# A fused recurrence and soft mixture of experts: the epsilon and the maximum's spread by reduces, slot factors on ScalarE, and identity transposes from less idle time on

## The chip, the cores and the metric

The kernel runs on one core of a Trainium2 chip. The metric is the device time of one execution in microseconds. Engines are called as in the profile: PE (TensorE; PEld its weight loads), DVE (VectorE), ACT (ScalarE), POOL (GpSimd), SP (SyncE, which issues the transfers). L1703 is line 1703 of the kernel before.

## The reference

Two layers, one behind the other. Cut to what matters:

```python
# 1. gated linear recurrence, x, r_gate, i_gate: 4 x 5056 x 256
a_t = np.exp(8.0 * sigmoid(r_gate) * np.log(clip(sigmoid(a_param))))
x_g = np.sqrt(np.maximum(1.0 - a_t * a_t, 1e-06)) * sigmoid(i_gate) * x
h = a_t[:, t] * h + x_g[:, t]          # over the 5056 steps of each batch; y[:, t] = h
# 2. soft mixture of experts over the 20224 tokens y, 8 experts x 4 slots = 32 slots
logits = y @ phi
d = np.exp(logits - logits.max(0)); d /= d.sum(0) + 1e-09      # over tokens
slot_input = d.T @ y
slot_out[e] = np.maximum(slot_input[e] @ w1[e], 0.0) @ w2[e]   # hidden width 1024
c = np.exp(logits - logits.max(1)); c /= c.sum(1) + 1e-09      # over slots: the combine
out = c @ slot_out
```

## The kernel before, in words

The 20224 tokens are cut into 40 pieces q of 512 (the last has 256), and the pieces into units p of one or two; channels lie on partitions in two halves h. For each piece, SP loads the tiles of r, i and x (Dr, Di, Dx); TensorE transposes r (TR, L879); ScalarE takes its tanh (SR, L887); an exponential makes the decay (EX, L994); GpSimd squares it (SQ, L976); ScalarE takes the root (RT, L1016) and the tanh of i (SI, L928); GpSimd multiplies gate and x (U, L956); TensorE transposes the products (TU, L1061); VectorE combines them (ST, L1077) and runs the scan (SC, L1094). TensorE then transposes the result back (TY, L1126), VectorE or ScalarE copies it out of PSUM (YC, L1141 or L1139; the last pieces in halves, L1167), and for groups g of up to four pieces TensorE computes the logits (LG), which are kept, and accumulates the slot inputs (AC, L1304) under a running maximum per group position (LE; AE adds into accS; DM is the factor for an older maximum).

When the last group is in, a thread of small steps joins the four rows of partial maxima and sums: MT transposes the maxima, MX (L1512) takes the maximum over the four, MR (L1514) spreads it over four places, MC (L1516) brings it back to the partitions by a product, WJ (L1518) subtracts, WE (L1521) takes the exponential, W (L1522) multiplies a constant 0/1 matrix R by it, SP0 and SP1 (L1528) join the sums with W, DN (L1542) the denominator, SL (L1539) copies the slots out. RD (L1546 to L1548) takes the reciprocal of the denominator and multiplies R by it to R2, which is used after the second expert layer (RS). L1.0 to L1.7 (L1583) and L2.0 to L2.7 (L1631) are the expert layers; HS and HR stand between them; HZ (L1559) and SZ (L1497) are memsets of their padded operands on GpSimd.

The combine weights are made for each group g: CT (L1681) transposes the logits to tokens on partitions, CM and CS (L1692, L1695) take off the maximum, CE (L1698) is the exponential, RR sums the slots (L1702), adds 1e-9 (L1703) and takes the reciprocal (L1704), CN (L1709) multiplies on GpSimd. Then HP (L1747) transposes, HE copies, OT (L1775) multiplies by the experts' outputs, OE (L1789 on ScalarE, L1791 on VectorE) copies the result out, and OD (L1806) stores it.

The order of the tasks on each engine is written out by hand (ORDER). A planner walks through these lists with a duration for each task, gives out the buffers at its planned times, and puts in identity transposes (two of a constant matrix, L1455; "fillers") where TensorE has nothing to do: up to the planned time 200 and again from 250 to 275, if a PSUM buffer is to spare. Up to 250 it also takes the last free buffer once a count of idle time is over the first number of DEBT; the count is capped by the second number, and TensorE's work pays it off at the rate of the third:

```python
self.debt = min(DEBT[1], self.debt + max(0.0, now - free_at[e]))
self.debt = max(0.0, self.debt - DEBT[2] * (extra + dur))
...
t = self.filler(now, now < self.warm_again and self.debt + now - free_at[e] > DEBT[0])
```

SHARED names the tasks on VectorE that the planner holds until GpSimd is free, and during which it holds GpSimd. SPX adds to the planned duration of single transfers on SP. Neither is an instruction. On VectorE the list around the thread is "LE11 LD11 AE9 MX MR RR2 WJ YC39.1 W AE11a AE11b CM4 SL CS4 RD RR4 RR1", on TensorE "TE10 TY39.1 MC AC10.0 AC10.1 AC11.0 CT4 SP0 SP1 DN L1.0", on ScalarE "ES11 YC39.0 WE DM10 CE4 HS0 HS1".

Of the kernel before, what the change touches and what calls it, by code (L numbers as in the profile page):

```python
# [16 lines left out]
P = 128  # L17
# [105 lines left out]
        EX18.1 DM6 YC28.0 SI37 DM8 RT18.0 YC30.0 YC29.0 RT20.0 YC31.0 YC29.2 RT19.0 YC32.0 ES8 YC34.0 CE1 YC33.0 YC35.0 YC38.0 YC37.0 YC36.0  # L123
        DM9 ES9 YC38.1 YC37.1 ES10 ES11 YC39.0 WE DM10 CE4 HS0 HS1 SO0 SO1 SH0 SH1 HE1.8 HE1.0 OE0.0 OE0.3 OE0.2 OE1.0 OE1.2 CE3 OE1.10
        HE2.0 HE2.8 OE1.11 CE11 OE1.9 OE2.0 OE2.3 CE8 OE2.1 OE2.8 OE2.9 HE4.0 OE2.11 CE5 OE2.10 HE4.8 OE4.0 OE4.1 OE4.2 CE10 OE3.0 OE3.3
# [10 lines left out]
        ST16.0 YC26.0 SC16.0 ST16.1 ST17.0 SC16.1 SC17.0 LE8 ST17.1 AE6 SC17.1 AE7 ST18.0 ST18.1 SC18.0 SC18.1 ST19.0 ST19.1 SC19.0 AE8 LE9  # L136
        SC19.1 ST20.1 ST20.0 SC20.1 SC20.0 LE10 RR0 LE11 LD11 AE9 MX MR RR2 WJ YC39.1 W AE11a AE11b CM4 SL CS4 RD RR4 RR1 HR0 HR1 HE0.0 CM3
        CS3 OE0.1 OE1.1 OE1.3 OE1.8 CM11 CS11 CM8 CM5 CS8 RR3 OE2.2 CS5 CM10 CM7 HE3.0 CS7 RR11 CS10 OE4.3 RR5 OE3.2 RR10 HE5.8 CM9 HE5.0
# [19 lines left out]
COLD = 5.5  # L158
DEBT = (1.2, 1.6, 0.8)

TT = 0.0622
HP = 64
SHARED = ("W", "MR", "RD", "U0", "SQ0.0", "SQ0.1")
RSEED = 523661183.0
# [51 lines left out]
class Planner:  # L216
# [158 lines left out]
    def run_fixed(self, orders):  # L375
# [32 lines left out]
        def begin(t, e):  # L408
            nonlocal n
            for b in t.alloc:  # L410
                self.take(b)
            dur, extra = t.alt.get(e, t.dur), 0.0
            if e == "PE":
                if self.shape is not None and t.shape != self.shape:
                    extra = SWITCH
                self.shape = t.shape
                if now < COLD:
                    dur *= 2
                self.debt = min(DEBT[1], self.debt + max(0.0, now - free_at[e]))
                self.debt = max(0.0, self.debt - DEBT[2] * (extra + dur))  # L420
            if e == "ACT" and t.kind and self.table not in KIND[t.kind]:
                extra = LOAD
                self.table = KIND[t.kind][0]
            if t.name == "LN":
                self.table = "exp"
            t.start, t.eng_used = now, e
            free_at[e] = now + extra + dur
            t.end = free_at[e] + t.lat
            order.append(t)
            n += 1  # L430
            heapq.heappush(finish, (t.end, n, t))

        while n_done < len(self.tasks):
# [17 lines left out]
            while again:  # L451
                again = False
                for e in engines:
# [12 lines left out]
                    if e == "PE" and (self.warm_from <= now < self.warm_to or self.warm_again <= now < self.warm_end):  # L466
                        t = self.filler(now, now < self.warm_again and self.debt + now - free_at[e] > DEBT[0])
                        if t is not None:
                            begin(t, e)
# [127 lines left out]
def kernel(  # L597
# [126 lines left out]
    def e_const():  # L724
# [777 lines left out]
    def merge_tasks():  # L1502
        small = {}
        if tc is not None:
            for nm, sh in (("mmax", [1, 1, NS]), ("mrep", [1, J, NS]), ("wj", [P, 1]), ("W", [P, J, NS]),
# [7 lines left out]
            out=small["mmax"][:, 0, :], in_=t(mp)[:1, :P].rearrange("o (j s) -> o s j", s=NS), axis=AX.X, op=ALU.max))  # L1513
        a = add("DVE", "MR", 0.21, deps=[a], prio=-60, emit=lambda: nc.vector.tensor_copy(  # L1514
            out=small["mrep"], in_=small["mmax"].broadcast_to([1, J, NS])))
        a = add("PE", "MC", 0.3, deps=[a], prio=-60, uses=[mp], shape="R", emit=lambda: nc.tensor.matmul(  # L1516
            t(mp)[:, P : P + 1], small["mrep"].rearrange("o j s -> o (j s)"), ones, start=True, stop=True))
        a = add("DVE", "WJ", 0.15, deps=[a], prio=-60, uses=[mp], emit=lambda: nc.vector.tensor_tensor(  # L1518
            out=small["wj"], in0=mm, in1=t(mp)[:, P : P + 1], op=ALU.subtract))
        a = add("ACT", "WE", 0.1, deps=[a], prio=-60, kind="exp",  # L1520
                emit=lambda: nc.scalar.activation(small["wj"], small["wj"], AF.Exp))  # L1521
        w = add("DVE", "W", 0.3, deps=[a, t_const2], prio=-60, emit=lambda: nc.vector.tensor_scalar(  # L1522
            small["W"], R, small["wj"], None, op0=ALU.mult))
        sp = Buf("one", "sp")
# [142 lines left out]
    def mk_c(g, first):  # L1667
# [177 lines left out]
```

## Time and profile before

| | us |
|---|---|
| median of 3 runs | 290.21 (290.15 to 290.63) |
| the profiled execution | 289.1 |
| its span, first to last instruction | 287.2 |
| busy PE / DVE / ACT / POOL | 247.3 / 233.1 / 236.1 / 189.7 |
| mean granted clock of TensorE | 0.988 of full |

The span is what the trace shows; the 1.9 us around it are launch and end. A busy share is a mean over stages with different limits, so the stages have to be read one by one. TensorE's busy time holds the fillers (L1455, 310 instructions).

### The profile page before, as it was taken

To read this page: it belongs to the slowest core of one execution; us is meant where nothing else is said; L and a number is where in the kernel's file an instruction comes from. 1 tells how busy PE (TensorE), PEld (TensorE's weight loads), DVE (VectorE), ACT (ScalarE), POOL (GpSimd) and SP (SyncE) were. 2 spreads that over 40 slices of the span, in tenths; PEclk is the share of its full clock that TensorE was granted. 3 is DMA by queue.
4 is the path that set the end of the run, shared out by engine and by line. 5 is a ranking of instruction groups with operands and counts; after the bars stand their busy time and mean duration, and the time that the engine had idled before them with its cause. 6 is when DMAs were issued, how large, how long until landed. Compare 5 with 4: busy or idle time off the path is not lost. (4 is left out here: it accounts for less than half of the span.)

```text
span 287.2 us, 9134 instructions
## 1 busy us (share of the span) xinstructions
PE 247.3 (86%) x3915; PEld 182.0 (63%) x3915; DVE 233.1 (81%) x275; ACT 236.1 (82%) x258; POOL 189.7 (66%) x144
## 2 busy tenths in 40 slices
PE   8978978998879879777987978989989999889980
PEld 7767665865645856656656746456545687667880
DVE  0896499999999999999999999999982189974600
ACT  7879999999999999999999999997511199868600
POOL 1458969999999999979999999991514002420000
PEclk9979999999999999999999999999999999999997
DMA  6999999999997799999899997999992069998995
GB/s 198 403 410 401 408 376 411 407 404 407 407 408 283 226 389 388 346 321 406 288 338 369 379 390 232 400 400 402 394 386 85 2 256 413 415 415 333 412 418 234
DMA packets 27421, 100.25 MB, mean 349 GB/s; under 512 B 3058, under 2 KB 3060, under 8 KB 24948
## 3 DMA queue, kind: packets, MB, share of 16 engines
q1 hardware_dynamic: 27376, 99.66, 89.8%
q8 instruction: 31, 0.51, 0.7%
q14 instruction: 10, 0.08, 0.1%
q10 hardware_dynamic: 4, 0.00, 0.0%
HBM read 78.94 MB, written 20.71 MB: 347 GB/s over the span
## 5 line engine op out<-in xcount | busy, mean ns | idle before, releaser
L956 POOL TENSOR_TENSOR b<-b 128x1024 f32<-128x1024 f32 x38 | 89.5, 2381 | 4.7 <-ACT b L928 4.2
L1094 DVE TENSOR_TENSOR_SCAN b<-b,pair 128x1024 f32<-128x1024 f32 (+8 forms) x48 | 92.3, 1948 | 0.2
L976 POOL TENSOR_TENSOR b<-b 128x1024 f32<-128x1024 f32 (+2 forms) x41 | 73.5, 1814 | 15.3 <-ACT b L994 14.6
L1077 DVE SCALAR_TENSOR_TENSOR pair<-b,pair 128x1024 f32<-128x1024 f32 (+2 forms) x42 | 48.1, 1156 | 5.6 <-ACT b L1016 3.8
L1061 PE MATMUL pair<-ident,b 64*128 64x64 f32 x1112 | 43.5, 226 | 5.9 <-ACT b L887 2.0
L1061 PEld LDWEIGHTS pair<-ident,b 64*128 64x128 f32 x1112 | 38.3, 139 | 13.9 <-issue 4.1
L994 ACT ACTIVATE b<-b,ca 128x2048 f32<-128x2048 f32 (+3 forms) x26 | 42.9, 1683 | 0.1
L887 ACT ACTIVATE b<-pair 128x1024 f32<-128x1024 f32 (+1 forms) x39 | 38.8, 1010 | 2.7 <-PE pair L879 2.7
L879 PE MATMUL pair<-ident,st 64*128 64x64 f32 x616 | 27.4, 230 | 11.3 <-DMA st<-in_r_gate_dram 4.4
L879 PEld LDWEIGHTS pair<-ident,st 64*128 64x128 f32 x616 | 22.5, 140 | 21.3 <-ACT b L887 5.0
L1016 ACT ACTIVATE b<-b 128x2048 f32<-128x2048 f32 (+1 forms) x20 | 35.9, 1842 | 0.1
L1709 POOL TENSOR_TENSOR b<-b,rs_all 128x512 f32<-128x512 f32 (+3 forms) x12 | 10.5, 895 | 37.4 <-DVE rs_all L1704 32.0
L928 ACT ACTIVATE b<-b 128x2048 f32<-128x2048 f32 x17 | 32.5, 1915 | 0.1
L1126 PE MATMUL pair<-ident,b 64*128 64x64 f32 x576 | 25.4, 227 | 7.1 <-DVE b L1094 3.2
L1126 PEld LDWEIGHTS pair<-ident,b 64*128 64x128 f32 x576 | 20.8, 138 | 16.8 <-DVE b L1094 4.6
L1141 DVE COPY yn<-pair 128x1024 f32<-128x1024 f32 x23 | 27.9, 1215 | 2.6 <-PE pair L1126 2.6
L1775 PE MATMUL bank<-eS,yn 32*128 32x256 f32 x238 | 26.4, 403 | 0.8 <-DVE yn L1760 0.4
L1789 ACT COPY b<-bank 128x512 f32<-128x512 f32 x41 | 22.4, 606 | 4.1 <-issue 2.5
L1304 PE MATMUL one<-yn,eS 128*32 128x257 f32 x316 | 24.2, 386 | 0.9 <-DVE yn L1167 0.9
L1455 PE MATMUL one<-ident 128*128 128x128 f32 x144 | 24.2, 284 | 0.3 <-DVE b L1219 0.3
L1206 PE MATMUL one<-b,phi_sb 128*32 128x512 f32 (+1 forms) x164 | 24.3, 581 | 0.0
L1775 PEld LDWEIGHTS bank<-eS,yn 32*128 32x128 f32 x238 | 19.4, 197 | 3.8 <-ACT b L1789 1.5
(156 smaller groups left out, 371.1 us busy)
## 6 DMA issues: line engine op xcount, KB each, us to landing
b<-in_x_dram SPq DMA_DIRECT2D x39, 512.0 KB, 9.0
st<-in_r_gate_dram SPq DMA_DIRECT2D x38, 512.0 KB, 9.1
b<-in_i_gate_dram SPq DMA_DIRECT2D x38, 512.0 KB, 8.5
out_dram<-b SPq DMA_DIRECT2D x19, 1024.0 KB, 6.3
b<-in_moe_w_dram SPq DMA_DIRECT2D x28, 512.0 KB, 8.8
st<-in_moe_w_dram SPq DMA_DIRECT2D x4, 512.0 KB, 7.7
st<-in_r_gate_dram SPq DMA_DIRECT2D x3, 256.0 KB, 2.8
st<-in_i_gate_dram SPq DMA_DIRECT2D x1, 512.0 KB, 5.4
```

Source lines behind the costliest of these rows:

```text
L879: nc.tensor.transpose(out=o[f][:, m, :], in_=v, identity=idn)
L887: nc.scalar.activation(dst, v, AF.Sigmoid if SIGR else AF.Tanh, scale=1.0 if SIGR else 0.5)
L928: nc.scalar.activation(v, v, AF.Tanh, scale=0.5)
L956: eng.tensor_tensor(out=o, in0=a, in1=b, op=ALU.mult)
L976: eng.tensor_tensor(out=o, in0=v, in1=v, op=ALU.mult)
L994: nc.scalar.activation(v, v, AF.Exp, scale=ca[:, h : h + 1], bias=ca[:, h : h + 1])
L1016: nc.scalar.activation(v, v, AF.Sqrt, bias=f, scale=-f)
L1061: nc.tensor.matmul(o[f][:, i * J + m, :], v, idn, is_transpose=True, start=(nm == nms[0] and m == 0 and i == 0), stop=(nm == nms[-1]), ski ...
L1077: nc.vector.scalar_tensor_tensor(v, t(Nb[p])[:, h, :c], 0.5e-3 if gate_of(quads(p)[0]) == "E" else 1e-3, v, op0=ALU.max, op1=ALU.mult)
L1094: nc.vector.tensor_tensor_scan(dst, dst, flat()[:, s0:s1], init, op0=ALU.mult, op1=ALU.add)
L1126: nc.tensor.transpose(out=t(yp)[:, f, (b * H + h) * HP : (b * H + h + 1) * HP], in_=v, identity=idn)
L1775: nc.tensor.matmul(t(ops[x])[:, c * D : (c + 1) * D], t(hT)[r, off : off + (P - 1) * ns + 1 : ns], t(soRb)[r, :D], start=True, stop=True,)
```

## The change

RR's addition of 1e-9 becomes a tensor_reduce: the sum is written beside a constant 1e-9 in a new tile rs_two, and a second reduce adds the pair. MR becomes a tensor_reduce over groups of one element. W leaves VectorE: WE and W become one task on ScalarE, the exponential and a copy of R scaled by it. R2 becomes a task of its own on ScalarE, between HS0 and HS1. In the planner, the count's numbers become 0.3 (limit) and 1.5 (rate) up to the planned time 45, then 1.0 and 1.0, where they were 1.2 and 0.8; W, MR and RD are no longer held for GpSimd; and planned durations of three transfers change.

```diff
-        DM9 ES9 YC38.1 YC37.1 ES10 ES11 YC39.0 WE DM10 CE4 HS0 HS1 SO0 ...
+        DM9 ES9 YC38.1 YC37.1 ES10 ES11 YC39.0 W DM10 CE4 HS0 R2 HS1 SO0 ...
-        SC19.1 ST20.1 ... MX MR RR2 WJ YC39.1 W AE11a AE11b CM4 SL CS4 RD ...
+        SC19.1 ST20.1 ... MX MR RR2 WJ YC39.1 AE11a AE11b CM4 SL CS4 RD ...
-DEBT = (1.2, 1.6, 0.8)
+DEBT = (1.0, 1.6, 1.0)
+DEBT0 = (45.0, 0.3, 1.5)
-SHARED = ("W", "MR", "RD", "U0", "SQ0.0", "SQ0.1")
+SHARED = ("U0", "SQ0.0", "SQ0.1")
-SPX = {("r", 0): 0.21, ("r", "b"): 0.33, ("r", 1): 0.45, ("r", 2): 0.32, ("r", 3): 0.1, ("x", PHI): 1.2}
+SPX = {("r", 0): 0.21, ("r", "b"): 0.33, ("r", 1): 0.45, ("i", 0): 0.55, ("x", PHI): 1.2}
-                self.debt = max(0.0, self.debt - DEBT[2] * (extra + dur))
+                self.debt = max(0.0, self.debt - (DEBT0 if now < DEBT0[0] else DEBT)[2] * (extra + dur))
-                        t = self.filler(now, now < self.warm_again and self.debt + now - free_at[e] > DEBT[0])
+                        t = self.filler(now, now < self.warm_again and self.debt + now - free_at[e] > (DEBT0[1] if now < DEBT0[0] else DEBT[0]))
+        rs_two = sb.tile([P, J * J, 2], F32, name="rs_two")
+        nc.gpsimd.memset(rs_two, 1e-9)
-        a = add("DVE", "MR", ... nc.vector.tensor_copy(
-            out=small["mrep"], in_=small["mmax"].broadcast_to([1, J, NS])))
+        a = add("DVE", "MR", ... nc.vector.tensor_reduce(
+            out=small["mrep"], in_=small["mmax"].rearrange("o j (s k) -> o j s k", k=1).broadcast_to([1, J, NS, 1]), axis=AX.X, op=ALU.max))
-        w = add("DVE", "W", 0.3, ... nc.vector.tensor_scalar(small["W"], R, small["wj"], None, op0=ALU.mult))
+        def e_we():
+            nc.scalar.activation(small["wj"], small["wj"], AF.Exp)
+            nc.scalar.activation(small["W"].rearrange("p j s -> p (j s)"), R.rearrange("p j s -> p (j s)"), AF.Copy, scale=small["wj"])
+        w = add("ACT", "W", 0.42, ... emit=e_we)
-            nc.vector.tensor_scalar(small["R2"], R.rearrange("p j s -> p (j s)"), small["rd"], None, op0=ALU.mult)
+        rd = add("ACT", "R2", 0.25, deps=[rd], ... nc.scalar.activation(
+            small["R2"], R.rearrange("p j s -> p (j s)"), AF.Copy, scale=small["rd"]))
-            nc.vector.tensor_reduce(out=v, in_=cn(), axis=AX.X, op=ALU.add)
-            nc.vector.tensor_scalar(v, v, 1e-9, None, op0=ALU.add)
+            nc.vector.tensor_reduce(out=rs_two[:, :m, 0], in_=cn(), axis=AX.X, op=ALU.add)
+            nc.vector.tensor_reduce(out=v, in_=rs_two[:, :m, :], axis=AX.X, op=ALU.add)
             nc.vector.reciprocal(v, v)
```

## Rows read from the trace of the kernel before

**Rows 1.** Windows of three stages: length, busy time (instructions) by engine, clock, DMA.
```profile
60.00:80.00 20.00, 17.06 (x308) 13.10 (x308) 19.95 (x20) 19.94 (x16) 19.38 (x11) 1.00 1.03 407
...
221.00:229.00 8.00, 8.00 (x131) 4.89 (x124) 0.69 (x3) 0.43 (x2) 0.00 (x0) 1.00 0.01 2
...
259.00:261.00 2.00, 2.00 (x15) 1.52 (x12) 0.59 (x2) 1.56 (x4) 0.00 (x0) 1.00 0.53 221
```

**Rows 2.** Timeline, 204 to 213 us: start, length, engine, line [idle before].
```profile
204.83 0.28 DVE L1702 TENSOR_REDUCE rs_all<-b 128x4 f32<-128x128 f32 x1
...
206.93 0.67 DVE L1702 TENSOR_REDUCE rs_all<-b 128x16 f32<-128x512 f32 x1
...
207.30 1.80 POOL L1559 MEMSET b<- 128x2048 f32 x1
...
207.63 1.97 DVE L1703 TENSOR_SCALAR rs_all<-rs_all 128x16 f32<-128x16 f32 x1
...
208.00 0.38 PE L1516 MATMUL bank<-ones,mrep 1*128 1x1 f32 x2
...
208.32 1.07 PE L1304 MATMUL one<-yn,eS 128*32 128x257 f32 x16
...
209.05 0.52 POOL L1497 MEMSET yn<- 128x512 f32 x1
...
209.63 0.25 DVE L1704 RECIPROCAL rs_all<-rs_all 128x16 f32<-128x16 f32 x1
...
209.80 0.10 DVE L1518 TENSOR_TENSOR wj<-M,bank 128x1 f32<-128x1 f32 x1
...
209.81 0.42 DVE L1167 COPY yn<-bank 128x256 f32<-128x256 f32 x1
...
210.25 0.29 DVE L1522 TENSOR_SCALAR W<-R,wj 128x128 f32<-128x128 f32 x1
...
210.28 0.63 PE L1304 MATMUL one<-yn,eS 128*32 128x257 f32 x4 [0.89 <-DVE yn L1167]
...
210.84 0.75 PE L1681 MATMUL bank<-ident,b 128*128 128x128 f32 x4
...
211.04 0.61 DVE L1338 SCALAR_TENSOR_TENSOR accS<-accS,dm,one 128x128 f32<-128x128 f32 x2 [0.50 <-PE one L1304]
...
211.53 0.60 PE L1528 MATMUL bank<-W,accS 128*64 128x32 f32 x8
```

**Rows 3.** Timeline, 248 to 258 us, the output stage.
```profile
248.49 1.05 POOL L1709 TENSOR_TENSOR b<-b,rs_all 128x512 f32<-128x512 f32 x1 [3.26 <-DVE rs_all L1704]
...
248.92 0.64 DVE L1703 TENSOR_SCALAR rs_all<-rs_all 128x16 f32<-128x16 f32 x1
...
254.73 1.53 PE L1455 MATMUL bank<-ident 128*128 128x128 f32 x12
...
257.40 0.59 ACT L1789 COPY b<-bank 128x512 f32<-128x512 f32 x1 [2.52 <-issue]
```

**Rows 4.** One line, L1141: duration min/median/max in ns, first and last start.
```profile
L1141 DVE COPY yn<-pair x23: 1198/1216/1226, 28.0 to 172.1; 128x1024 f32<-128x1024 f32 x23
```

**Rows 5.** Windows of 1 and 0.5 us at the fall of the clock.
```profile
15.00:16.00 1.00, 0.11 (x4) 0.00 (x0) 0.81 (x2) 1.00 (x2) 1.00 (x1) 1.00 1.00 406
...
18.00:18.50 0.50, 0.50 (x12) 0.50 (x13) 0.47 (x2) 0.40 (x1) 0.10 (x1) 0.50 1.06 426
```

**Rows 6.** Timeline, 17 to 24 us, TensorE and ScalarE.
```profile
16.63 0.71 PE L879 MATMUL pair<-ident,st 64*128 64x64 f32 x16 [1.52 <-DMA st<-in_r_gate_dram]
...
17.90 1.11 PE L879 MATMUL pair<-ident,st 64*128 64x64 f32 x16 [0.56 <-DMA st<-in_r_gate_dram]
...
19.06 1.03 ACT L887 ACTIVATE b<-pair 128x1024 f32<-128x1024 f32 x1 [0.65 <-PE pair L879]
...
19.80 3.66 PE L1455 MATMUL pair<-ident 128*128 128x128 f32 x26
```

**Rows 7.** Waits from 40 to 206 us: total us, times, longest.
```profile
ACT yn L1139 <- PE pair L1126: 1.7, 2, 1.1
```

More of the change, by code (lines that the diff above doesn't have):

```diff
@@ L123 @@
         EX18.1 DM6 YC28.0 SI37 DM8 RT18.0 YC30.0 YC29.0 RT20.0 YC31.0 YC29.2 RT19.0 YC32.0 ES8 YC34.0 CE1 YC33.0 YC35.0 YC38.0 YC37.0 YC36.0
-        DM9 ES9 YC38.1 YC37.1 ES10 ES11 YC39.0 WE DM10 CE4 HS0 HS1 SO0 SO1 SH0 SH1 HE1.8 HE1.0 OE0.0 OE0.3 OE0.2 OE1.0 OE1.2 CE3 OE1.10
+        DM9 ES9 YC38.1 YC37.1 ES10 ES11 YC39.0 W DM10 CE4 HS0 R2 HS1 SO0 SO1 SH0 SH1 HE1.8 HE1.0 OE0.0 OE0.3 OE0.2 OE1.0 OE1.2 CE3 OE1.10
         HE2.0 HE2.8 OE1.11 CE11 OE1.9 OE2.0 OE2.3 CE8 OE2.1 OE2.8 OE2.9 HE4.0 OE2.11 CE5 OE2.10 HE4.8 OE4.0 OE4.1 OE4.2 CE10 OE3.0 OE3.3
@@ L136 @@
         ST16.0 YC26.0 SC16.0 ST16.1 ST17.0 SC16.1 SC17.0 LE8 ST17.1 AE6 SC17.1 AE7 ST18.0 ST18.1 SC18.0 SC18.1 ST19.0 ST19.1 SC19.0 AE8 LE9
-        SC19.1 ST20.1 ST20.0 SC20.1 SC20.0 LE10 RR0 LE11 LD11 AE9 MX MR RR2 WJ YC39.1 W AE11a AE11b CM4 SL CS4 RD RR4 RR1 HR0 HR1 HE0.0 CM3
+        SC19.1 ST20.1 ST20.0 SC20.1 SC20.0 LE10 RR0 LE11 LD11 AE9 MX MR RR2 WJ YC39.1 AE11a AE11b CM4 SL CS4 RD RR4 RR1 HR0 HR1 HE0.0 CM3
         CS3 OE0.1 OE1.1 OE1.3 OE1.8 CM11 CS11 CM8 CM5 CS8 RR3 OE2.2 CS5 CM10 CM7 HE3.0 CS7 RR11 CS10 OE4.3 RR5 OE3.2 RR10 HE5.8 CM9 HE5.0
@@ L1513, in merge_tasks @@
             out=small["mmax"][:, 0, :], in_=t(mp)[:1, :P].rearrange("o (j s) -> o s j", s=NS), axis=AX.X, op=ALU.max))
-        a = add("DVE", "MR", 0.21, deps=[a], prio=-60, emit=lambda: nc.vector.tensor_copy(
-            out=small["mrep"], in_=small["mmax"].broadcast_to([1, J, NS])))
+        a = add("DVE", "MR", 0.21, deps=[a], prio=-60, emit=lambda: nc.vector.tensor_reduce(
+            out=small["mrep"], in_=small["mmax"].rearrange("o j (s k) -> o j s k", k=1).broadcast_to([1, J, NS, 1]), axis=AX.X, op=ALU.max))
         a = add("PE", "MC", 0.3, deps=[a], prio=-60, uses=[mp], shape="R", emit=lambda: nc.tensor.matmul(
@@ L1519, in merge_tasks @@
             out=small["wj"], in0=mm, in1=t(mp)[:, P : P + 1], op=ALU.subtract))
[L1520 to L1523, printed above, removed]
+        def e_we():
+            nc.scalar.activation(small["wj"], small["wj"], AF.Exp)
+            nc.scalar.activation(small["W"].rearrange("p j s -> p (j s)"), R.rearrange("p j s -> p (j s)"), AF.Copy, scale=small["wj"])
+        w = add("ACT", "W", 0.42, deps=[a, t_const2], prio=-60, kind="exp", emit=e_we)
         sp = Buf("one", "sp")
@@ L1547, in e_rd @@
             nc.vector.reciprocal(small["rd"], small["rd"])
-            nc.vector.tensor_scalar(small["R2"], R.rearrange("p j s -> p (j s)"), small["rd"], None, op0=ALU.mult)
-        rd = add("DVE", "RD", 0.5, deps=[a], prio=-10, uses=[sp], emit=e_rd)
+        rd = add("DVE", "RD", 0.3, deps=[a], prio=-10, uses=[sp], emit=e_rd)
+        rd = add("ACT", "R2", 0.25, deps=[rd], prio=-10, emit=lambda: nc.scalar.activation(
+            small["R2"], R.rearrange("p j s -> p (j s)"), AF.Copy, scale=small["rd"]))
         return small, sl, rd
```

## The prediction

> **What bounds the kernel now.** I read the windows of the span first, then the chain that ended last, then the timeline at the places that the diff touches, and last the waits. In the windows the reader is to see three stages. From about 38 to 206 us ScalarE, VectorE and GpSimd are full together: in 60 to 80 us they are busy 19.94, 19.95 and 19.38 of 20 us, while TensorE has 2.9 us free [rows 1]. From 206 to 229 us one thread of small dependent steps and then the two expert layers run, TensorE without a gap and DMA at 0.01 [rows 1]. From 231 us on outputs leave, DMA nearly always full, but at 0.53 in 259 to 261 us [rows 1]. So three places can give time: the start, which shifts the full stage; the thread at 206 to 213 us, which nothing covers; and pauses of the output DMA. The chain names many TensorE steps at its end that are identity transposes; they fill idle time and say nothing of the bound.
>
> **The thread at 206 us: epsilon and maximum.** The reduction of RR2 ends at 207.60. The small L1703 behind it, 16 numbers a partition, takes 1.97 us, to 209.60 [rows 2]. During all of it GpSimd runs two memsets, 207.30 to 209.10 and 209.05 to 209.57; L1703 ends 0.03 us behind the second [rows 2]. I read this as a wait inside the instruction for what GpSimd holds. A second case agrees: L1703 at 248.92 takes 0.64 us and ends at 249.56, GpSimd's multiply at 249.54 [rows 3]. The reduction itself did not wait: it began at 206.93, ran 0.37 us beside the first memset and took 0.67 [rows 2]. So a reduce in L1703's place should not wait either.
>
> Behind L1703 on VectorE are queued the reciprocal (0.25), WJ (0.10) and the copy YC39.1 (0.42, to 210.23) [rows 2]. For that copy TensorE waits 0.89 us with AC11, then come CT4, AE11 on VectorE, and SP0 at 211.53 [rows 2].
>
> The new step sums two numbers for each of 16 outputs, 32 elements. No row has it. Below, it costs nothing; above, the 0.28 us of the reduce that reads 128 elements. Between 128 (0.28) and 512 (0.67) an element costs 1.0 ns [rows 2], so 32 come to 0.28 - 0.10 = 0.18, which I take. RR2 then ends near 207.62 + 0.18 + 0.25 and two small gaps, 208.1. WJ also needs the product MC, which ends at 208.38 [rows 2]; this is late next. I put WJ at 208.46, and the copy at 208.56 to 208.98. The copy reads PSUM; copies of that kind took 1198 to 1226 ns, 23 times, in a stage where GpSimd is full [rows 4], so I cost it no wait. TensorE is in AC10 until 209.39 [rows 2], and AC11 follows without its 0.89 us pause. Its four products took 0.63 after a pause; sixteen in a row took 1.07 [rows 2], so four cost 0.27 to 0.63 behind them. AC11 ends at 209.66 to 210.02, against 210.91: gain 0.89 to 1.25, and I take 1.05. CT4, AE11, SP0 and the expert layers follow in the same order on engines with nothing else to do, so SP0 moves from 211.53 to about 210.48 and the 1.05 stays.
>
> The spread of the maximum as a reduce: nothing to 0.28 us more (the 128-element row); all of it added, MR still ends at 207.21, and MC begins at 208.00 behind other TensorE work [rows 2]. Cost nothing; without that cover, up to 0.28.
>
> [...]
>
> **The slot factors on ScalarE.** W leaves VectorE (0.29 [rows 2]) and follows the exponential on ScalarE, with DM10, CE4 and HS0 queued behind. No row has such a scaled copy; nothing to 0.59 (a 128x512 copy, [rows 3]) each for exponential and scaling, and I take 0.3, near the 0.29 of the same shape. W ends at 208.56 + 0.6 = 209.2, at worst 209.75, before SP0 at 210.48; DM10 follows by 209.5, or 210.05 at worst, which would hold AE11 by some 0.1. R2 leaves VectorE too and stands on ScalarE between HS0 and HS1; its readers come after the second layer, which still runs at 229 [rows 1]. Both cost nothing while that cover stands.
>
> **Earlier identity transposes.** [...] The r transposes at 17.90 take 1.11 us, those at 16.63 took 0.71 [rows 6]. ScalarE waits 0.65 us for them and starts SR6 at 19.06 [rows 6], one of its last waits before it is full. At the full clock they end 0.40 earlier and SR6 moves to 18.66, still behind the pass before it, which ends at 18.41 (19.06 - 0.65). The gap before 16.63 is where a threshold of 0.3 instead of 1.2 us lets transposes in. An identity transposition in front of a landed tile costs up to 0.26 us (1.53 / 6, two instructions each [rows 3]). So the gain is 0 to 0.40 if the clock holds, -0.26 at worst if it doesn't; I take 0.35. GpSimd and VectorE get their inputs from ScalarE, so a start 0.35 earlier moves the full stage as a whole. The new limits of SP's planned times change no order of transfers, only where the planner sees idle time. The memset of the epsilon tile lies in the first 2 us, before GpSimd has inputs.
>
> **The output stage.** Without the wait at 248.92 VectorE has 0.64 - 0.18 = 0.46 us back. At 254.73 twelve identity instructions hold TensorE for 1.53 us, and ScalarE then idles 2.52 us to 257.40 [rows 3]; the DMA loses 0.47 x 2 = 0.94 us in 259 to 261 [rows 1]. VectorE's copies could come earlier there and the pause shrink: 0 to 0.94, and I take 0.25, since the burst may still stand in front.
>
> **Sum.** 1.05 + 0.35 + 0.25 = 1.65 us. The profiled execution took 289.1 (span 287.2 and 1.9 around it), so it would be 287.45. The median of the timed runs is 1.1 higher, 290.21; the same gain there gives 288.56, rounded to 288.6.
>
> **Rivals.** *The clock falls all the same*, because the transposes land beside the gap: no 0.35, 290.21 - 1.30 = 288.9. For it: the planner's time is not the chip's. Against: the gap is long and empty [rows 5].
>
> *The reciprocal takes the wait.* It is the next small instruction on the same 16 numbers; both times it started only after GpSimd was done (209.63, and behind 249.56), so no row shows it beside a busy GpSimd. If it waits to 209.57, WJ stays near 209.8 and the thread gives nothing, nor does 248.92: 290.21 - 0.35 = 289.9. [...]
>
> *The output stage gives it back.* Identity transposes there start at a fixed time of the plan, 250 us; in a shorter plan they meet other work, and another burst of 1.53 us [rows 3] at a moment when DMA has nothing queued costs about what the thread gains: 290.21 - 1.65 + 1.53 = 290.1, or 289.7 if half is covered.
>
> *Slower: transposes in the full stage.* From 45 us on the limit falls from 1.2 to 1.0 us. A transposition put in right before a tile becomes ready costs ScalarE or VectorE 0.26 us, and there it is not made good, since they are full. The gain is eaten by 1.65 / 0.26 = 6 of them, and slower by over 0.2% needs 9; ten give 290.21 - 1.65 + 2.6 = 291.2. Against: over 160 us ScalarE's largest wait for TensorE is 1.7 us in two times [rows 7], and TensorE has 15% free.
>
> **Numbers.** A measurement of this kernel tells no change from about 0.2%, 0.6 us. Forecast 0.54; clock falls 0.20; reciprocal 0.09; output stage 0.09 (0.04 of it still faster); full stage 0.08. Faster 0.54 + 0.20 + 0.04 = 0.78, same 0.09 + 0.05 = 0.14, slower 0.08. The low end takes the upper bounds, 1.25 + 0.40 + 0.94 = 2.59: 287.6. The high end takes in the reciprocal and the output rival: 290.1. Outside lies mainly the slower case.
>
> **What the changed profile would show.** Right: a reduce near 0.18 us in L1703's place beside the memset, WJ near 208.5 less any earlier shift, AC11 without a pause, clock at 1.00 through 18 to 21 us, SR6 0.3 to 0.4 earlier. Wrong: a long reciprocal; a clock of 0.5 there; new waits of ScalarE or VectorE for TensorE between 40 and 206 us; a DMA share under 0.5 in more output windows than one.

## The result and the profile after

| | before | after |
|---|---|---|
| median | 290.27 us (290.15 to 290.69, 6 runs) | 286.81 us (284.52 to 288.82, 6 runs) |
| ratio | | 0.9859, 95% interval 0.9824 to 0.9895 |
| the profiled execution, its span | 289.1, 287.2 | 284.5, 282.7 |

The change gives 3.5 us, twice the forecast, and the time lies 0.8 us under the forecast range. The ratio, here and below, leaves out executions more than 1.5% above the fastest of their kernel, so it is not the quotient of the medians. The profiled execution of after is also the fastest of its six, so the two spans lie 4.5 us apart. Lines of the kernel after stand 3 to 5 further down than in before (L1703 is L1708, L1522 is L1525).

A warning ahead of the reading: single executions of most of the kernels below lie 2 to 5 us apart, and in 35 runs of before on one chip 0.01 of mean granted clock went with 1.6 us on the mean. A median of 6 to 12 runs therefore carries about 0.4%; parts of a microsecond have to be read as distances inside the traces.

**The thread at 206 us.** The first step of the thread, MX, in before, then the timeline of after (start, length, engine, line):

```profile
206.49 0.27 DVE L1512 TENSOR_REDUCE mmax<-bank 1x32 f32<-1x128 f32 x1
```

```profile
204.70 0.27 DVE L1515 TENSOR_REDUCE mmax<-bank 1x32 f32<-1x128 f32 x1
...
205.21 0.66 DVE L1707 TENSOR_REDUCE rs_two<-b 128x16 f32<-128x512 f32 x1
205.45 1.81 POOL L1564 MEMSET b<- 128x2048 f32 x1
...
205.91 0.19 DVE L1708 TENSOR_REDUCE rs_all<-rs_two 128x16 f32<-128x32 f32 x1
206.13 0.25 DVE L1709 RECIPROCAL rs_all<-rs_all 128x16 f32<-128x16 f32 x1
206.15 0.38 PE L1519 MATMUL bank<-ones,mrep 1*128 1x1 f32 x2
...
206.47 1.50 PE L1307 MATMUL one<-yn,eS 128*32 128x257 f32 x20
206.56 0.16 DVE L1521 TENSOR_TENSOR wj<-M,bank 128x1 f32<-128x1 f32 x1 [0.18 <-PE bank L1519]
...
206.84 0.43 DVE L1170 COPY yn<-bank 128x256 f32<-128x256 f32 x1
207.05 0.40 ACT L1525 ACTIVATE W<-R,wj 128x128 f32<-128x128 f32 x1
...
208.09 0.61 DVE L1341 SCALAR_TENSOR_TENSOR accS<-accS,dm,one 128x128 f32<-128x128 f32 x2 [0.83 <-PE one L1307]
208.58 0.60 PE L1532 MATMUL bank<-W,accS 128*64 128x32 f32 x8
```

The new reduce and the reciprocal both run inside GpSimd's memset (205.45 to 207.26) at 0.19 and 0.25 us. WJ now waits 0.18 for the product. TensorE's twenty products run through where sixteen and four stood apart by 0.89 us [rows 2]. From MX (204.70) to SP0 (208.58) it is 3.88 us; in before it was 206.49 to 211.53 [rows 2], 5.04. So 1.16 us come from here.

**The output stage.** The first output transfer in before, then the timeline of after, then its windows at and ahead of the place of the pause in before:

```profile
231.55 0.36 SPq L1806 DMA_DIRECT2D out_dram<-st  x1
```

```profile
228.61 0.36 SPq L1811 DMA_DIRECT2D out_dram<-st  x1
...
250.27 0.66 PE L1458 MATMUL one<-ident 128*128 128x128 f32 x4 [0.30 <-ACT yn L1763]
...
252.94 0.59 ACT L1794 COPY b<-one 128x512 f32<-128x512 f32 x1 [1.02 <-issue]
```

```profile
255.00:257.00 2.00, 2.00 (x12) 1.38 (x11) 0.76 (x2) 1.44 (x4) 0.00 (x0) 1.00 0.99 410
...
259.00:261.00 2.00, 2.00 (x29) 1.55 (x24) 1.53 (x3) 2.00 (x5) 0.00 (x0) 1.00 0.96 401
```

Four identity instructions stand where twelve held TensorE for 1.53 us [rows 3]; ScalarE's idle time there is 1.02 instead of 2.52 us, and from 231 to 279 us no window of 2 us has a DMA share under 0.90. From the first output transfer to the end of the span it is 282.7 - 228.61 = 54.09 us, against 287.2 - 231.55 = 55.65.

**The full stage.** Groups of one line by shape, the exponentials of the decay, first before, then after (count, busy us, mean ns):

```profile
L994 ACT ACTIVATE b<-b,ca 128x2048 f32<-128x2048 f32 x16 | 33.2, 2097 | 0.0
L994 ACT ACTIVATE b<-b,ca 128x1024 f32<-128x1024 f32 x6 | 7.1, 1234 | 0.0
```

```profile
L997 ACT ACTIVATE b<-b,ca 128x2048 f32<-128x2048 f32 x18 | 37.3, 2094 | 0.0
L997 ACT ACTIVATE b<-b,ca 128x1024 f32<-128x1024 f32 x2 | 2.4, 1235 | 0.0
```

The diff does not touch this line, and yet two exponentials of 2048 stand in place of four of 1024. The same work takes 2 x (2 x 1.235 - 2.094) = 0.75 us less on ScalarE, which is full there (busy 2.00 of 2.00 us in 106 to 108 us). On the timeline, before and after, the two places are near 102 and 106 us:

```profile
103.10 2.38 ACT L994 ACTIVATE b<-b,ca 128x1024 f32<-128x1024 f32 x2
105.38 1.91 ACT L887 ACTIVATE b<-pair 128x1024 f32<-128x1024 f32 x2
107.19 2.36 ACT L994 ACTIVATE b<-b,ca 128x1024 f32<-128x1024 f32 x2
```

```profile
102.40 2.10 ACT L997 ACTIVATE b<-b,ca 128x2048 f32<-128x2048 f32 x1
104.40 1.92 ACT L890 ACTIVATE b<-pair 128x1024 f32<-128x1024 f32 x2
```

The cause is in the kernel's source: one exponential spans two units only if their buffers lie at most 15 apart, and the planner gives buffers out at its planned times. With the old numbers unit 10 got buffer 1 and unit 11 buffer 18; with the new ones 1 and 4.

**The start.** Timeline and windows of after:

```profile
16.55 0.71 PE L882 MATMUL pair<-ident,st 64*128 64x64 f32 x16 [0.17 <-DMA st<-in_r_gate_dram]
...
17.30 1.02 ACT L890 ACTIVATE b<-pair 128x1024 f32<-128x1024 f32 x1 [0.49 <-PE pair L882]
```

```profile
18.00:18.50 0.50, 0.24 (x3) 0.12 (x2) 0.47 (x2) 0.47 (x2) 0.00 (x0) 1.00 0.99 377
24.00:26.00 2.00, 1.01 (x17) 0.93 (x16) 1.38 (x2) 2.00 (x2) 2.00 (x2) 0.74 1.02 418
26.00:28.00 2.00, 2.00 (x30) 1.60 (x28) 0.00 (x0) 1.84 (x3) 1.06 (x2) 0.50 1.04 412
```

The second r transposition takes 0.71 us instead of 1.11 [rows 6], the clock is 1.00 at 18 us instead of 0.50 [rows 5], and SR6 starts at 17.30 instead of 19.06. But most of this is the landing of the r tiles: the second transposition starts at 16.55 instead of 17.90, 1.35 us earlier, and at 16.63 the clock of before had not fallen either (0.71 us, [rows 6]). The clock fell all the same, 7 us later, and by the exponential near 42 us only 0.72 of the 1.76 us are left (41.72 against 42.44).

So the 4.5 us between the two spans are 0.72 to 42 us, 0.86 from there to the last exponential of 2048 (135.50 instead of 136.36), 0.21 to MX, 1.16 in the thread, 1.56 in the output stage.

### The profile page after: what moved, and what is told of

It reads as the page before. It is cut to its first block, busy times and chain, and to the rows that moved or that the text cites. A ratio compares the mean times of both kernels' runs of the same rounds, so it can differ in the third digit from the quotient of the medians.

```text
span 282.7 us, 9139 instructions
## 1 busy us (share of the span) xinstructions
PE 248.3 (88%) x3915; PEld 182.1 (64%) x3915; DVE 230.2 (81%) x273; ACT 235.8 (83%) x258; POOL 189.5 (67%) x145
## 4 chain that ended last, share of the span: by engine, by line
PE 37%; DVE 19%; DMA 16%; POOL 10%; issue 9%; ACT 6%; DVEq 0%; ACTq 0%; POOLq 0%
DVE b L1097 8%; DMA st<-in_r_gate_dram 7%; POOL b L959 6%; DVE pair L1080 5%; PE bank L1780 5%; DMA b<-in_x_dram 4%; PE pair L1064 3%; DVE yn L1144 3%; PE bank L1458 3%; DMA b<-in_i_gate_dram 3%; PE one L1307 3%; POOL b L979 3%; PE one L1458 3%; PE bank L1636 2%; DMA st<-in_moe_w_dram 2%
## 5 line engine op out<-in xcount | busy, mean ns | idle before, releaser
L997 ACT ACTIVATE b<-b,ca 128x2048 f32<-128x2048 f32 (+3 forms) x24 | 42.3, 1790 | 0.1
L1458 PE MATMUL one<-ident 128*128 128x128 f32 x154 | 26.8, 288 | 2.4 <-DVE b L1043 1.7
L1780 PE MATMUL bank<-eS,yn 32*128 32x256 f32 x238 | 24.7, 401 | 0.5 <-DVE yn L1765 0.4
L1794 ACT COPY b<-bank 128x512 f32<-128x512 f32 x43 | 23.2, 603 | 1.8 <-PE bank L1780 1.5
L1458 PEld LDWEIGHTS one<-ident 128*128 128x128 f32 x154 | 17.4, 144 | 6.3 <-DVE b L1043 1.9
```

The source lines that it names most:

```text
L997: nc.scalar.activation(v, v, AF.Exp, scale=ca[:, h : h + 1], bias=ca[:, h : h + 1])
L1458: nc.tensor.transpose(out=t(b)[:, 0, :P] if b.tag == "pair" else t(b)[:, :P], in_=ident, identity=ident)
L1780: nc.tensor.matmul(t(ops[x])[:, c * D : (c + 1) * D], t(hT)[r, off : off + (P - 1) * ns + 1 : ns], t(soRb)[r, :D], start=True, stop=True,)
```

## The experiments

My first theory was: thread 1.16 us, the vanished burst 1.5, the rest from the earlier identity transposes. The main rivals were that the output stage gains through VectorE's shorter wait, and that the rest is scatter. The table has every run. *42* is the start of the exponential near 42 us, *full* the way from it to the start of the last exponential of 2048, *thread* MX to SP0, *out* the first output transfer to the end of the span, each from the one profiled execution; the times are medians, with before from the same chip.

| | time | before | ratio (95%) | 42 | full | thread | out |
|---|---|---|---|---|---|---|---|
| before | | | | 42.44 | 136.36 | 5.04 | 55.65 |
| after | 286.81 | 290.27 | 0.9859 (0.9824-0.9895) | 41.72 | 135.50 | 3.88 | 54.09 |
| e1_again | 286.08 | 289.84 | 0.9887 (0.9851-0.9923) | 41.82 | 135.65 | 3.87 | 54.06 |
| e2_noburst | 288.16 | 289.84 | 0.9947 (0.9910-0.9985) | 43.27 | 136.04 | 5.05 | 53.95 |
| e3_thread | 288.18 | 289.84 | 0.9955 (0.9922-0.9988) | 42.33 | 136.04 | 3.88 | 55.32 |
| e4_plan | 287.17 | 289.84 | 0.9921 (0.9889-0.9953) | 42.57 | 135.52 | 5.04 | 54.24 |
| e5_burst_back | 286.15 | 290.12 | 0.9893 (0.9830-0.9955) | 41.30 | 135.52 | 3.87 | 55.37 |
| e6_no_out_fill | 286.31 | 290.12 | 0.9869 (0.9811-0.9928) | 42.22 | 136.79 | 3.88 | 53.58 |
| e7_late_limit | 286.35 | 290.12 | 0.9880 (0.9821-0.9939) | 41.37 | 136.78 | 3.89 | 53.94 |
| e8_eps_scalar | 288.10 | 290.12 | 0.9937 (0.9899-0.9974) | | | | |
| e9_split | 286.67 | 289.75 | 0.9919 (0.9888-0.9950) | 43.30 | 136.20 | 3.87 | 54.11 |
| e10_near | 287.84 | 289.75 | 0.9919 (0.9883-0.9955) | 41.78 | 135.66 | 5.04 | 54.03 |
| e11_parts | 287.26 | 289.75 | 0.9891 (0.9837-0.9946) | 42.89 | 137.19 | 3.89 | 53.98 |
| e12_eps_again | 287.69 | 289.75 | 0.9952 (0.9918-0.9987) | 42.69 | 138.61 | 4.96 | 54.32 |
| e13_limit150 | 285.75 | 289.64 | 0.9872 (0.9837-0.9907) | 41.38 | 138.11 | 3.87 | 53.45 |
| e14_no_out_near | 284.84 | 289.64 | 0.9838 (0.9800-0.9875) | 41.52 | 135.56 | 3.87 | 54.03 |
| e15_parts_again | 285.18 | 289.64 | 0.9846 (0.9806-0.9886) | 41.81 | 135.46 | 3.89 | 53.96 |
| e16_limit45 | 286.66 | 289.64 | 0.9888 (0.9841-0.9935) | | | | |
| e17_after_again | 285.50 | 290.64 | 0.9867 (0.9816-0.9918) | 42.13 | 135.60 | 3.88 | 54.18 |
| e18_no_out_again | 285.87 | 290.64 | 0.9867 (0.9814-0.9921) | 43.12 | 136.23 | 3.88 | 53.66 |

The profiles of e8_eps_scalar and e16_limit45 come from disturbed executions and give no distances (the last section has them).

### The change in halves

e1_again is after unchanged. The three others against before or after (cut: the SPX line changes with them, and in e4 the two lines that use DEBT0):

```diff
# e2_noburst: before with
-WARMA = 250.0
+WARMA = 252.5
# e3_thread: after with the planner numbers of before
-DEBT = (1.0, 1.6, 1.0)
-DEBT0 = (45.0, 0.3, 1.5)
+DEBT = (1.2, 1.6, 0.8)
+DEBT0 = (0.0, 0.3, 1.5)
...
# e4_plan: before with the planner numbers of after
+DEBT = (1.0, 1.6, 1.0)
+DEBT0 = (45.0, 0.3, 1.5)
...
```

> The changed kernel once more, unchanged. Its timed runs spread from 284.5 to 288.8 us, where those of before lie within 0.6 us. Theory A (the start differs from run to run: the fifth r tile landed at 14.9 us in the profiled execution of after and at 16.5 us in that of before): this profile shows another landing time, SR6 starting somewhere between 17.3 and 19.1 us, and its own time moves with it by as much. Theory B (the early landing belongs to the change): SR6 again at 17.3 us within 0.2. In both the thread from AE9 to SP0 takes 4.3 us (5.44 before) and the pause of the output transfers at 259 us is gone.

> The kernel before with one number changed: identity transposes in the output stage start at the planned time 252.5 instead of 250, which takes out the six that stood between OT9.0 and OT9.8. If this burst caused the pause of the output transfers at 259 to 261 us, the stage from the first output to the end shortens by 0.7 to 1.5 us and the time falls to 288.8 to 289.6. If the pause has another cause (buffers, the multiplies on GpSimd), the time stays at 290.2 within 0.4.

> The changed instructions alone (epsilon and maximum by reduce, W and R2 on ScalarE), with the planner's old numbers, so the same order, buffers and identity transposes as before. By the step of the prediction: 1.05 us from the thread, 289.2, and 0 to 0.4 more from the epsilon in the output stage; the burst at 254 us and the pause at 259 us stay. If instead the whole gain hangs on the instructions: 286.8. If the reciprocal waits for GpSimd in L1703's place: 290.2.

> The planner's new numbers alone, with the old instructions: the same order, buffers and identity transposes as after. The wait of L1703 behind the memsets stays, so SP0 comes 5.4 us after AE9. If start and output stage make the difference of 3.4 us less the thread's 1.2: 288.0 (287.4 to 288.6), with the clock falling after 22 us instead of at 17.8 and the output pause gone. By the prediction's sizes (0.35 at the start, nothing in the output stage): 289.9.

The thread is 3.88 us with the new instructions and 5.04 with the old ones, whatever the plan (e3, e4). The output stage is 55.3 to 55.7 with the old plan and 54.1 to 54.2 with the new one, whatever the instructions: so VectorE's shorter wait in that stage is not what takes off the 1.4 us. Moving only the start of the window (e2) gives 53.95. In the medians e3 gives 1.7 and e4 2.7 us, together 4.4 beside the 3.8 of e1, which is the same within their scatter. SR6 of e1 starts at 17.57, near the 17.3 of after, so its two theories stay undecided by this one profile. The new plan also has a *full* of 135.5 to 135.7 where the old one has 136.04 to 136.36, which I first took for the work of the identity transposes.

### The burst put back, and the output stage without identity transposes

```diff
# e5_burst_back: after with
-WARMA = 250.0
+WARMA = 250.7
# e6_no_out_fill: after with
-WARMA = 250.0
+WARMA = 300.0
-WARME = 275.0
+WARME = 300.0
```

> The kernel after, with the window of the output-stage identity transposes opened at 250.7 us of the plan instead of 250.0, so that six of them stand together behind OT9.0 again, as they did in the plan of before. Theory (the output part of the gain is that burst, and it came out because a longer plan reached OT9.0 after the window had opened): thread and start as in after, MX to SP0 3.9 us, and from the first output transfer to the end of the span about 55.5 us instead of 54.1, with a pause of the output DMA near 260 us; time 1.3 to 1.6 us above after. Rival (the output stage is shorter because VectorE has its wait back or because the stage starts earlier): 54.1 us again, and the time of after.

> The kernel after with no identity transposes at all in the output stage (none behind 200 us of the plan, 50 fewer). Theory A (they are only in the way there, since the DMA sets that stage): from the first output transfer to the end 54.0 us or less, time as after or up to 0.3 us below. Theory B (they hold TensorE's clock up there and the output transposes need it): a granted clock of 0.5 in parts of the stage, real transposes twice as long, pauses of the DMA, 55 us or more, and the time 1 us or more above after.

Timeline and window of e5_burst_back:

```profile
251.43 1.53 PE L1458 MATMUL bank<-ident 128*128 128x128 f32 x12
...
254.10 0.59 ACT L1794 COPY b<-bank 128x512 f32<-128x512 f32 x1 [2.38 <-issue]
```

```profile
255.00:257.00 2.00, 2.00 (x15) 1.61 (x15) 0.43 (x1) 1.56 (x5) 0.00 (x0) 1.00 0.53 217
```

Opening the window 0.7 us later is enough to bring back all three marks of before: twelve identity instructions in 1.53 us, ScalarE idle 2.38, DMA at 0.53. *out* is 55.37. The planner shows why: with the old numbers it puts OT9.0, the output product ahead of the burst, at 249.38 us, before the window at 250 opens, and six identity transposes then stand behind it; with the new numbers two stand in front of it and it starts at 250.53. The trace bears the theory out; the median doesn't show it (286.15 beside 286.31 and 286.35 of the two others on its chip, where 1.3 more were expected; its interval is 3.6 us wide).

Without any identity transposes (e6) the stage is not longer: the clock stays at 1.00 until 270 us, and *out* is 53.58. So they aren't needed there.

### The epsilon by itself

```diff
-            nc.vector.tensor_reduce(out=rs_two[:, :m, 0], in_=cn(), axis=AX.X, op=ALU.add)
-            nc.vector.tensor_reduce(out=v, in_=rs_two[:, :m, :], axis=AX.X, op=ALU.add)
+            nc.vector.tensor_reduce(out=v, in_=cn(), axis=AX.X, op=ALU.add)
+            nc.vector.tensor_scalar(v, v, 1e-9, None, op0=ALU.add)
```

> The kernel after with the epsilon added by the scalar addition of before again, behind the reduction; all else as in after, the plan too. Theory (the thread's gain is the wait of that one instruction for GpSimd): it takes about 2 us beside GpSimd's memset, MX to SP0 goes from 3.88 back to about 5.0 us, time 1.1 us above after. Rival (the slot factors on ScalarE or the maximum carry part of it): MX to SP0 between 4.0 and 4.7 us, time 0.2 to 0.8 us above after.

> The kernel of e8_eps_scalar once more, for its trace, which was of a run of 535 us with TensorE at half its pace and can't be read. Theory: the scalar addition takes about 2 us beside GpSimd's memset, MX to SP0 5.0 us, time 1.1 us above after (e8_eps_scalar: 1.9 above the mean of the three others of its chip). Rival (the slot factors or the maximum carry part): MX to SP0 between 4.0 and 4.7 us.

Timeline of e12_eps_again:

```profile
209.72 1.81 POOL L1564 MEMSET b<- 128x2048 f32 x1
...
210.19 1.83 DVE L1708 TENSOR_SCALAR rs_all<-rs_all 128x16 f32<-128x16 f32 x1
...
211.47 0.52 POOL L1500 MEMSET yn<- 128x512 f32 x1
...
212.05 0.25 DVE L1709 RECIPROCAL rs_all<-rs_all 128x16 f32<-128x16 f32 x1
...
212.71 0.63 PE L1307 MATMUL one<-yn,eS 128*32 128x257 f32 x4 [0.89 <-DVE yn L1170]
```

The scalar addition takes 1.83 us and ends 0.03 behind the second memset; TensorE's pause of 0.89 is back to the digit. The thread is 4.96 us, so this one instruction carries 1.08 of the 1.16; the slot factors and the maximum together carry at most 0.08. In the medians e8 stands 1.75 to 1.95 us above the three others of its chip, which have the reduce, and e12 1.0 above e9_split, which has the reduce but split exponentials.

### The limit before 45 us

```diff
# e7_late_limit: after with
-WARMA = 250.0
+WARMA = 252.5
-DEBT0 = (45.0, 0.3, 1.5)
+DEBT0 = (0.0, 0.3, 1.5)
```

> The kernel after with the lower limit before 45 us taken back (1.0 us of idle time there as in the rest of the plan; three fewer early identity transposes, none at 16.3 us of the plan), and the window of the output stage moved to 252.5 us so that no burst forms. Theory (the early transposes give the start): the clock falls before or at the transposes of r6 as in before, or falls a second time near 40 us; the first maximum step is 0.4 to 0.8 us later than in after, thread and output stage as in after, time 0.4 to 0.8 us above after. Rival (the start of after comes from the earlier landing of the r tiles, or is scatter): the maximum step and the time as in after, within 0.3 us.

Its exponential near 42 us is as early as in after (41.37), so the start does not miss the early transposes. It loses 1.3 us later, in *full*, and part of that pointed to a cause: the plan of e7 also has unit 11 seventeen buffers from unit 10, and the exponentials at 102 and 106 us are split. Up to 100 us e7 and after differ in nothing but the limit before 45 us, so with the other new numbers in place it is this limit that decides the buffers. The split pair takes 0.56 of the 1.3 us; what took the rest, at 46 to 65 us and behind 130 us, is not shown.

### The two exponentials

```diff
# e9_split: after with
-            if len(us) == 2 and hi - lo > 15:
+            if len(us) == 2 and (hi - lo > 15 or p == 10):
# e10_near: e2_noburst with
         A[p].near = A[p - 1]
+        A[p - 1].near = A[p]
```

> The kernel after with the two exponentials of the units 10 and 11 (near 102 and 106 us) each split into two instructions of 128x1024 again, as in before, where the buffers of the two units lay 17 apart and one instruction could not span them; plan, order and all else as in after. Theory (ScalarE is full there, so its instructions set the pace): each split costs 2 x 1.235 - 2.094 = 0.38 us of ScalarE, the exponentials behind 140 us stand 0.5 to 0.75 us later against the one at 101 us than in after, thread and output stage as in after, time 0.5 to 0.75 us above after, which the medians may not tell from scatter, but the trace does. Rival (what the kernel before lost between 102 and 137 us came from the identity transposes of its plan): the distances of the exponentials stay as in after, within 0.1 us.

> The kernel before without the burst in the output stage (as e2_noburst) and with one more line by which unit 10 takes a buffer near that of unit 11: the plan is that of e2_noburst step for step, two buffers are swapped, and the two exponentials are one instruction each. Theory: 18 exponentials of 128x2048 instead of 16, and from 101 us to the exponential near 179 us the trace loses nothing against after (e2_noburst lost 0.55 us, before 0.7); MX to SP0 5.05, first output transfer to the end 54.0; time about 0.6 us below e2_noburst, 2.1 below before. Rival (the identity transposes): the same loss as in e2_noburst.

Timeline of e9_split, and the group of e10_near:

```profile
104.13 2.38 ACT L997 ACTIVATE b<-b,ca 128x1024 f32<-128x1024 f32 x2
106.41 1.91 ACT L890 ACTIVATE b<-pair 128x1024 f32<-128x1024 f32 x2
```

```profile
L995 ACT ACTIVATE b<-b,ca 128x2048 f32<-128x2048 f32 x18 | 37.3, 2095 | 0.0
L995 ACT ACTIVATE b<-b,ca 128x1024 f32<-128x1024 f32 x2 | 2.4, 1236 | 0.0
```

Splitting them under the plan of after lengthens the way from the exponential at 101 us on by 0.56 us; near buffers under the plan of before take *full* from 136.04 to 135.66, and nothing is lost behind 101 us. Over the profiles without a clock fall behind 43 us in this stage, the five with split exponentials (before, e2, e3, e7, e9) have 136.28 on the mean, the nine with whole ones 135.63 (after, e1, e4, e5, e10, e14, e15, e17, e18). Two of them lose time elsewhere, e7 as above and e18 with a wait of 0.47 us for an i tile at 49.71; without these two it is 136.16 and 135.56. So it is 0.6 of the 0.75 us that ScalarE saves, and e10, which has the identity transposes of the old plan, shows no other loss behind 46 us.

### All parts without the planner's new numbers

```diff
# e11_parts, e15_parts_again: e3_thread with
-WARMA = 250.0
+WARMA = 252.5
         A[p].near = A[p - 1]
+        A[p - 1].near = A[p]
# e16_limit45: the same with
-DEBT0 = (0.0, 0.3, 1.5)
+DEBT0 = (45.0, 0.3, 1.5)
```

> The instructions of after in the thread and on ScalarE, all planner numbers of before, and beside them only the window of the output stage at 252.5 us and the near buffers. Theory (the gain of after is the thread 1.16, the burst 1.5 and the two exponentials 0.55; the lower limits of the identity transposes and SP's planned times give nothing of their own): time as after, 3.2 us below before, within 0.5 us. Rival (the earlier identity transposes give the start 0.35 us or more): MX stands later than in after by that much in the trace beyond what clock falls explain, and the time 0.4 to 0.8 us above after.

> The same kernel as e11_parts: the instructions of after, the planner numbers of before, no burst, near buffers. Beside it e16_limit45 adds the lower limit before 45 us. Theory A (the lower limit gives the start 0.35 us or more on the mean, by fewer clock falls): this one 0.3 to 0.8 us above e16_limit45, mean granted clock lower by 0.002. Theory B (it gives nothing): the same within 0.3 us.

> e15_parts_again with the lower limit for identity transposes before 45 us of the plan, as in after (4 more there, at 16.0, 34.6, 35.9 and 43.9 us of the plan among them), and nothing else. Theory A: no clock fall at 38 to 43 us, the exponential near 42 us 0.4 us earlier than in e15_parts_again, time 0.3 to 0.8 below. Theory B: the clock falls as often as without, times the same within 0.3 us.

With the thread's instructions, no burst and whole exponentials, the planner's old numbers give 2.5 and 4.5 us (e11, e15), after on its chips 3.5, 3.8 and 5.1: the same within what such medians tell. Adding the limit before 45 us (e16) comes out 1.5 us higher, with overlapping intervals; theory A, 0.3 to 0.8 lower, has nothing for it, and theory B's 0.3 us can't be told either. e11's *full* of 137.19 holds a clock fall at 134 to 140 us.

### Clock falls in the full stage, and the last two

```diff
# e14_no_out_near, e18_no_out_again: after with
-WARMA = 250.0
+WARMA = 300.0
-WARME = 275.0
+WARME = 300.0
+        A[p - 1].near = A[p]
# e13_limit150: e14_no_out_near with
-DEBT0 = (45.0, 0.3, 1.5)
+DEBT0 = (150.0, 0.3, 1.0)
```

> The kernel after with the lower limit for early identity transposes (0.3 us of idle time) kept to 150 us of the plan instead of 45 (12 more of them between 45 and 150), and none in the output stage. Theory (the clock falls that some profiles show at 38 to 43, 106 to 110 and 134 to 140 us cost about 1 us each, and denser identity transposes keep them away): no fall of the granted clock between 30 and 206 us, output stage 53.6 us as in e6_no_out_fill, time 0.3 to 1 us below after. Rival (each added transpose delays VectorE or ScalarE, which are full): the exponentials behind 101 us stand 0.3 us or more later against the one at 42 us than in after without a clock fall, time as after or above.

> The same instructions as e6_no_out_fill (after without identity transposes in the output stage), on the chip and beside the runs of the kernel that it differs from only by the limit to 150 us. Theory: output stage 53.6 us, 0.5 less than after, time 0.3 to 0.5 us below after, so 3.6 to 4 below before. Rival (the clock is needed there): 54.1 or more.

> The kernel after, unchanged, beside e18_no_out_again on one chip. Both theories of that run: 3.3 to 3.5 us below before.

> The same kernel as e14_no_out_near. Theory (the output stage needs no identity transposes): 0.3 to 0.6 us below e17_after_again. Rival (it makes no difference, and the lower median of e14_no_out_near came from its chip and its few clock falls): within 0.3 us.

The added line gives the same buffers as after here, so e6, e14 and e18 are one program three times. With 13 more transposes in the full stage (e13; 236 identity instructions instead of 210) ScalarE waits 0.8 us for r transposes between 66 and 90 us and its exponentials come 0.88 later, with the clock at 1.00 there. Timeline of e13:

```profile
72.55 0.34 PE L1065 MATMUL pair<-ident,b 64*128 64x64 f32 x4 [0.61 <-issue]
...
75.12 1.02 ACT L891 ACTIVATE b<-pair 128x1024 f32<-128x1024 f32 x1 [0.79 <-PE pair L883]
```

That delay is of the size that the rival of e13 foretold; the time, 285.75 beside 285.50 of e17, tells nothing. But its mechanism is not shown: ahead of the wait TensorE pauses for 0.61 us in the middle of real products, and the last identity transposes stand 6 us before. The theory of e13 isn't borne out either: the clock falls at 164 to 170 us, behind the 150 up to which the limit held, and after, e1, e4, e5 and others have no fall between 43 and 206 us without the added transposes. e14 had the lowest median of all, though its *out* of 54.03 missed the 53.6 expected; beside after on one chip (e17, e18) the two kernels are alike, 285.50 and 285.87. Over the four profiles without identity transposes *out* is 53.68 on the mean, over the eleven with them and without the burst 54.08; that 0.4 us was not seen in the times. No version here beats after by what can be measured.

## Why the prediction was wrong

**The thread: right.** Predicted 1.05 of 0.89 to 1.25, measured 1.16: the thread takes 3.87 to 3.89 us in every undisturbed profile with the reduce. Each link held: the reduce 0.19 us (0.18 predicted), the copy beside GpSimd's memset without a wait (0.43), the four products behind the sixteen for 1.50 - 1.07 = 0.43. W takes 0.40 us and ends 1.1 us before SP0, R2 (0.41) runs at 213.87 under the expert layers: both nothing, as costed. At the same place beside the same memset the scalar addition takes 1.83 us (e12) and the reduce 0.19; why the one waits and the other does not, no run shows. The row from which the prediction took that a reduce does not wait was weaker than it says: the reduce of before ran 0.37 us ahead of the first memset and 0.30 beside it [rows 2], so it had begun before. The one of after begins inside the memset.

**The reciprocal takes the wait: false.** It takes 0.25 us in the middle of a memset, as behind one [rows 2].

**The output stage: this is the step that failed.** The prediction put 0.25 us on it, "since the burst may still stand in front", with 0.94 as the upper bound. It measured 1.56 between the two profiles, and 55.45 - 54.08 = 1.37 over the three profiles with the burst and the eleven with identity transposes but without it. Two things were wrong in it. The burst was taken as given, though its place depends on where a window, fixed at 250 us of the plan, opens against the work; the new numbers shift the work in the plan, and 0.7 us decide (e5). And the bound came from one pause of the DMA, 0.94 us in one window, where the removal of the burst was never priced: twelve instructions, 1.53 us [rows 3], behind which ScalarE idles for 2.52. Nor was that pause the only one: before also has the DMA at 0.78 in 265 to 267 us, up to 0.44 us. The term's own mechanism, VectorE's copies coming earlier with the burst still there, may be worth what was put on it: 55.65 in before against 55.32 and 55.37 in e3 and e5, one profile each. Without the burst the old and the new addition of epsilon differ by under 0.1 us in *out* on the mean.

**The output stage gives it back: false, with the wrong sign.** The rival had the mechanism, a fixed window that meets other work, but argued that a shift makes a burst. A burst was already there to lose. Its second figure is also a slip: half of 1.53 gives 290.21 - 1.65 + 0.77 = 289.3, not 289.7.

**No term for the full stage.** The prediction read the planner's numbers as changing "no order of transfers, only where the planner sees idle time". The planner gives out buffers too, and the width of two pairs of exponentials hangs on how far apart they lie: 0.6 us. The sum put nothing on it. Thread, burst and exponentials, 1.16 + 1.37 + 0.6 = 3.1, are most of the 3.5 us.

**The start: 0.35 not found.** What was to be seen was seen (SR6 1.76 us earlier, clock 1.00 at 18 us), but it does not recur with the limit: the exponential near 42 us starts at 42.16 on the mean of eleven profiles with the limit and at 42.27 of seven without, and each kind spreads from 41.3 to 43.3. That transposes in the gap ahead of the r tiles would keep the clock at 1.00 was the author's estimate; no run shows it. The early fall at 17 to 22 us, on which the term rests, is a matter of the execution: it stands in one of the seven without the limit, before itself, and in two of the eleven with it (e6, e12), while e14, the same program as e6, has none there. And in e4, which has the limit, the clock is at 1.00 until 279 us (0.990 on the mean of the span), and still the exponential stands at 42.57: there the clock bought nothing. That the profile of before shows the fall and the latest SR6 of all these profiles looks like chance. The rival "the clock falls all the same" describes it better than the forecast did. Whether the limit gives a tenth or two stays open; a second fall at 38 to 43 us, seen in 4 of the 7 profiles without the limit and 2 of the 11 with it, would be a reason why it should.

**Slower through the full stage: false.** ScalarE waits for TensorE at YC as in before [rows 7]; the larger wait in the list, 3.3 us at the last pieces, is no new one, in before it ends at 206.41 us and takes 3.27:

```profile
ACT yn L1168 <- PE bank L1158: 3.5, 2, 3.3
ACT yn L1142 <- PE pair L1129: 1.6, 2, 1.1
```

**A reading of the stages.** "TensorE without a gap and DMA at 0.01" holds for 221 to 229 us alone [rows 1]; in 206 to 221 us TensorE has gaps, the 0.89 us among them, and the DMA share is 0.77. No term rests on it.

## What to carry to other kernels

Where a planner places work by its own times, a change of its numbers is a change of buffers, widths and bursts everywhere; compare groups by shape and instruction counts per stretch between two builds before any timing, and price what such a reshuffle could remove as well as what it could add. A window fixed in planned time is fragile: look at what stands at both its edges. Look for long durations of small instructions beside another engine's work: here the scalar addition of 16 numbers a partition took 1.97 us beside GpSimd's memsets, and the reduce at its place took 0.19.

## What the hardware showed that was not expected

One and the same program meets clock falls at different places: ahead of the output stage e6, e14 and e18 (identical) fell at 16 to 22, 38 to 42 and 106 to 110 us, at 24 to 30 only, and at 22 to 32. The fall of e6 in the full stage is not hidden. Windows at 106 us, e6_no_out_fill and then after (second to last columns: granted clock, DMA share, GB/s):

```profile
106.00:108.00 2.00, 1.82 (x40) 1.67 (x38) 2.00 (x3) 2.00 (x2) 2.00 (x2) 0.64 1.02 389
108.00:110.00 2.00, 2.00 (x44) 2.00 (x42) 1.49 (x2) 2.00 (x2) 1.93 (x2) 0.50 1.00 404
```

```profile
106.00:108.00 2.00, 1.98 (x65) 1.88 (x61) 2.00 (x3) 2.00 (x2) 2.00 (x2) 1.00 1.03 416
108.00:110.00 2.00, 2.00 (x50) 1.33 (x49) 2.00 (x3) 2.00 (x2) 2.00 (x2) 1.00 1.03 416
```

At 0.50 VectorE is busy 1.49 of 2 us, and e6's exponentials stand 1.15 us later from there to the end of the stage.

Three executions ran wholly otherwise. One of e8_eps_scalar took 535 us at a mean granted clock of 1.00, where the eleven others took 286.5 to 291.9; one of e16_limit45 had a clock of 0.85, neither the 1.00 nor the 0.50 of the other profiles, nearly throughout from 7 us to the end and took 292.5 us; one of before, beside e17 and e18, took 429.75 us at a mean clock of 1.00 and left no trace. What caused them no run here shows.
